# Exponentials as 32-bit integers, split into float16 halves for the product with v

## The chip, the cores and the metric

The kernel runs on one core of one Trainium2 chip. The metric is the device time of one execution in microseconds (us), the median of several runs. Times inside an execution come from one profiled execution and its trace.

## What is computed

Two parts follow each other: block-sparse attention over 4 batches, 8 heads, 768 positions and a head width of 64, and a mixture of experts in which each of 3072 rows goes to its best two of 8 experts.

```python
scores = scale * np.matmul(q, k.transpose(0, 1, 3, 2))      # scale = 1/8
scores = np.where(mask, scores, -1000000000.0)               # blocks of 32 x 32
scores = scores - np.max(scores, axis=-1, keepdims=True)
attn = np.exp(scores)
attn = attn / (np.sum(attn, axis=-1, keepdims=True) + 1e-09)
attn_out = np.matmul(attn, v)                                # (4, 8, 768, 64)
x = attn_out.transpose(0, 2, 1, 3).reshape(3072, 512)
# experts: the top 2 of x @ w_gate + log1p(exp(x @ w_noise)) * noise, softmax over the two,
# out[rows] += weight * (relu(x[rows] @ w1[e]) @ w2[e])
```

The change touches attention only.

## The kernel before

**Stages.** Attention is a loop of 192 steps (`steps`, 4 batches x 8 heads x 6 key tiles of 128; two heads make a group, so a group is 12 steps and there are 16 groups). Then the experts run unit by unit. The router of a batch works in the background of the attention steps, and some loads and conversions of the first expert's weights lie in the last steps.

**One attention step** n belongs to one head and one tile c of 128 keys. TensorE forms the scores of these 128 keys against all 768 queries in two halves of 384 (`exp`, called with x = 0 and 1). Each half is two float16 products added in PSUM: line 237 (high part of k and q, with what the split of k left over) and line 238 (k again, with what the split of q left over, the block mask, and one row that carries minus the row maximum and the constant LNS). ScalarE turns each half into exponentials (line 239), 128 x 384 float32, into half of a tile p32 of 128 x 6 x 128.

Ahead of that, the row maxima of a later head are found: `max_mm` (line 208) makes two products of width 384 into one of two PSUM buffers pm, and VectorE reduces them (`max_red`, line 215). At a head's last tile `max_end` (line 222) writes minus the maximum into a column of the natural-layout tile qb, which SyncE transposes into q2 (line 225).

Three steps after its exponentials (LA = 3), a tile's p32 is multiplied with v (`av`, line 259): p32's six blocks of 128 x 128 are the stationary weights, v's 128 x 65 the moving side, in float32, summed over the head's six steps in one PSUM buffer po. Column 65 is a constant, so that it collects the denominator. Behind a head's last step `av_end` copies po out (ScalarE, line 271), adds the 1e-9 (line 274), inverts (276), scales (279), and splits the result into two float16 parts (ScalarE line 286, GpSimd line 288).

**Splits and loads.** q and k come in as float32 (line 154, ScalarE's queue) and are split into two float16 parts: high on ScalarE (lines 173 and 177), the rest on GpSimd (175 and 179). v is loaded straight into its float32 tile vx (line 149, two transfers of 192 KB a group, since vx has 65 columns where v has 64).

**What sets the order.** The program is written out in the order in which each engine runs it; `steps` is that order. Within a step TensorE has: first score half, maxima product, second score half, product with v; in a head's last step of v the product comes first. VectorE has: line 274 if due, the maximum, lines 276, 279 and 222 if due, with the router's small instructions between (`background`). Each engine takes its own list in order; the engines wait for one another through semaphores, and for buffers: 3 of pe (scores), 2 of pm (maxima), 1 of po, 5 of p32.

Of the kernel before, what the change touches and what calls it, by code (L numbers as in the profile page):

```python
# [9 lines left out]
F32 = mybir.dt.float32  # L10
F16 = mybir.dt.float16
BF16 = mybir.dt.bfloat16
I32 = mybir.dt.int32
U32 = mybir.dt.uint32
AF = mybir.ActivationFunctionType
ALU = mybir.AluOpType
AX = mybir.AxisListType
PSUM = bass.MemoryType.PSUM
P = 128


LNS = 12.0 * math.log(2.0)

XS = 64.0
WS = 64.0
# [14 lines left out]
class Attention:  # L40
    G = 2
# [6 lines left out]
    VLOADAT = 6  # L48

    SPLITAT = ((0, 0, 0), (1, 0, 1), (2, 1, 0), (5, 1, 1), (5, 2, None), (6, 3, None), (8, 4, None), (9, 5, None))  # L50
    PPB = 5
    LA = 3

# [13 lines left out]
    def open(self, ctx, early):  # L67

        tc, nc, G, T = self.tc, self.nc, self.G, self.T
        pool = lambda c, name, bufs, **kw: c.enter_context(tc.tile_pool(name=name, bufs=bufs, **kw))  # L70
        self.const = pool(ctx, "aconst", 1, side="right")
        self.tp = pool(ctx, "atp", 3, side="right")
        self.pp = pool(ctx, "app", self.PPB, side="right")
        self.sm = pool(ctx, "asm", 4, side="right")
        self.xp = pool(ctx, "axp", 2, side="right")
        self.ps_e = pool(ctx, "ps_e", 3, space=PSUM)
        self.ps_m = pool(ctx, "ps_m", 2, space=PSUM)
        self.ps_o = pool(ctx, "ps_o", 1, space=PSUM)
        self.natp = pool(ctx, "anat", 1, side="right")
        self.raw = pool(early, "araw", 2)  # L80
        self.nat = [tuple(self.natp.tile([P, G, T, P], F16, name=f"{n}{i}") for n in ("ka", "qa", "qb"))
                    for i in range(2)]
        self.k2 = [self.natp.tile([P, G, T, P], F16, name=f"k2{i}") for i in range(3)]

        self.vx = [self.natp.tile([P, G, T, self.D + 1], F32, name=f"vx{i}") for i in range(3)]
        for t in self.vx:
            nc.gpsimd.memset(t[:, :, :, self.D:], 1.0 / XS)

    def masks(self, mi, sb):

        nc, T, NB, G = self.nc, self.T, self.NB, self.G
# [6 lines left out]
                       allow_small_or_imprecise_dtypes=True)  # L98
        self.kb = mi.tile([P, G, T, P], F16, name="kb")
        nc.gpsimd.memset(self.kb[:, :, :, 64:], 0.0)  # L100
        nc.gpsimd.memset(self.kb[:, :, :, 64 + NB:65 + NB], 64.0)
        self.blank(0)
        nc.vector.tensor_scalar(rowi, rowi, 5, None, op0=ALU.arith_shift_right)
        rowb = mi.tile([P, T], F32, name="rowb")
# [28 lines left out]
    def blank(self, i):  # L133
        ka, qa, qb = self.nat[i]
        self.nc.gpsimd.memset(qa[:, :, :, 64 + self.NB:], 0.0)
        self.nc.gpsimd.memset(qb[:, :, :, 64 + self.NB:], 0.0)

    def blocks(self, i, k):
        for g in range(self.G):
# [2 lines left out]
    def load(self, g, eng=None, names="kq"):  # L142
        b, h0 = divmod(g * self.G, self.H)
        r = self.st.setdefault(g, {})
        for nm in names:
            if nm == "v":
                x = r["v"] = self.vx[g % 3]
                for h in range(self.G):
                    (eng or self.nc.scalar).dma_start(x[:, h, :, 0:self.D],
                                                      self.v[b, h0 + h].rearrange("(p t) d -> p t d", p=P))  # L150
                continue
            src = {"k": self.k, "q": self.q}[nm]
            x = self.raw.tile([P, self.G, self.T * self.D], F32, name="raw_" + nm)
            (eng or self.nc.scalar).dma_start(x, src[b, h0:h0 + self.G].rearrange("h (p t) d -> p h (t d)", p=P))
            r[nm] = x.rearrange("p h (t d) -> p h t d", t=self.T)

    def new(self, r, nm):
        r[nm] = self.tp.tile([P, self.G, self.T, P], F16, name=nm)
# [58 lines left out]
    def max_end(self, n):  # L217
        g, h, t = self.where(n)
        r = self.st[g]
        if t == self.T - 1:  # L220
            qb = self.nat[g % 2][2]
            self.nc.vector.tensor_scalar(qb[:, h, :, 64 + self.NB], r["m", h], -1.0 / 64.0, LNS / 8.0,
                                         op0=ALU.mult, op1=ALU.add)
            d = r["q2", h] = self.tp.tile([P, self.T, P], F16, name="q2", bufs=2)
            self.later(self.Q2LATE, lambda: self.nc.sync.dma_start_transpose(
                out=d, in_=qb[:, h].rearrange("p t c -> p (t c)")))

    def exp(self, n, x):
        nc, T = self.nc, self.T
        g, h, c = self.where(n)  # L230
        r = self.st[g]
        if x == 0:
            self.st["p", n] = self.pp.tile([P, T, P], F32, name="p32")
        p32 = self.st["p", n]
        t = slice(3 * x, 3 * x + 3)
        pe = self.psum()
        nc.tensor.matmul(pe[:, 0:384], r["k1"][:, h, c, :], r["q1"][:, h, t, :], start=True, stop=False)  # L237
        nc.tensor.matmul(pe[:, 0:384], r["k2"][:, h, c, :], r["q2", h][:, t, :], start=False, stop=True)  # L238
        nc.scalar.activation(p32[:, t].rearrange("p t c -> p (t c)"), pe[:, 0:384], AF.Exp, scale=0.125)  # L239

    def flush(self):
        for n in sorted(self.todo):
# [9 lines left out]
    def av(self, n):  # L252
        g, h, c = self.where(n)
        r = self.st[g]
        if c == 0:
            r["o", h] = self.ps_o.tile([P, self.T, self.D + 1], F32, name="po")
        po, p32 = r["o", h], self.st.pop(("p", n))
        for t in range(self.T):
            self.nc.tensor.matmul(po[:, t, :], p32[:, t, :], r["v"][:, h, c, :], start=(c == 0 and t == 0),  # L259
                                  stop=(c == self.T - 1 and t == self.T - 1), skip_group_check=True)  # L260

    def av_end(self, n, part, on_group):

        nc, T, D, G = self.nc, self.T, self.D, self.G
        if n < 0 or n >= self.NSTEP or n % T != T - 1:
            return
        g, h, c = self.where(n)
        r = self.st[g]
        if part == "copy":
            xo = r["xo", h] = self.sm.tile([P, T, D + 1], F32, name="xo", bufs=2)  # L270
            nc.scalar.activation(xo, r.pop(("o", h)), AF.Copy)  # L271
        elif part == "sum":
            r["rc", h] = self.sm.tile([P, T], F32, name="rc")
            nc.vector.tensor_scalar(r["rc", h], r["xo", h][:, :, D], 1e-9 * math.exp(LNS) / XS, None, op0=ALU.add)
        elif part == "inverse":
            nc.vector.reciprocal(r["rc", h], r["rc", h])
        elif part == "scale":
# [14 lines left out]
    def start(self, mi):  # L292
        nc, D, NB = self.nc, self.D, self.NB
# [4 lines left out]
        r = self.st[0] = {nm: self.raw.tile([P, self.G, self.T, D], F32, name="raw_" + nm) for nm in "kq"}  # L298
# [4 lines left out]
        ka, qa, qb = self.nat[0]  # L303
# [24 lines left out]
            self.max_end(n)  # L328
        self.flush()
        self.load(0, nc.scalar, "v")  # L330
        self.split(1, 3)
        self.split(1, 2)
        nc.sync.dma_start(self.k2[1][D:], self.k2[0][D:])
# [10 lines left out]
    def steps(self, on_group, background):  # L344
        NSTEP, LM, LA, GT = self.NSTEP, self.LM, self.LA, self.G * self.T
        for n in range(NSTEP + LA + 6 + self.ROWLATE):
            g, i = divmod(n, GT)
# [24 lines left out]
                self.av(j)  # L372
            background(n, 0)
            self.av_end(j - 1, "sum", on_group)
            background(n, 1)
            for m in new:
                self.max_red(m)
# [722 lines left out]
```

## Time and profile before

| | |
|---|---|
| runs shown | 1116.45 us median of 3 (1113.26 to 1122.55) |
| profiled execution: span from the first to the last instruction | 1064.2 us |
| the profiled execution's own time | not recorded beside its span; the median of the runs is 52 us above it |
| attention: first and last product with v | 32.3 and 469.7 us |
| experts | from 469.9 us |
| granted TensorE clock, mean | 0.986 |
| DMA traffic | 156.24 MB, mean 147 GB/s |

How to read the rows. Engines are PE (TensorE's matmuls), PEld (its weight loads, which overlap PE), DVE (VectorE), ACT (ScalarE), POOL (GpSimd), SP (SyncE). A group's row gives line, engine, operation, tiles written and read, shape, count, busy us and mean ns of one, and then the idle time in front of it with what ended it. A timeline row gives start, length, engine, line, operation. A row of a stretch gives its limits and length, the busy us of the engines with their counts, the granted clock, the share of the 16 DMA engines and GB/s. A matmul's length includes a modelled end, so the pace of matmuls is read from their starts. A float32 matmul of the program is recorded as two loads and two matmuls.

### The profile page before, as it was taken

The numbers are of one execution on the slowest core, as the hardware profiler recorded it, in microseconds if no ns is written. First come the engines' busy times: TensorE is split into PE (matmuls) and PEld (weight loads), VectorE is DVE, ScalarE is ACT, GpSimd is POOL, SyncE is SP. The second block draws the span as 40 slices with busy tenths as digits, with TensorE's granted clock in tenths as the row PEclk, the third lists the DMA queues.
The fourth block names the chain that finished last, engine by engine and source line by source line (L and its number), as shares of the span: only waits on it lengthen the run. The fifth ranks groups of instructions, "written<-read, shape, count | busy, mean of one in ns | idle before, by whom it ended". The sixth has DMA issues, their size and how long they took to land. (4 is left out here: it accounts for less than half of the span.)

```text
span 1064.2 us, 18061 instructions
## 1 busy us (share of the span) xinstructions
PE 998.3 (94%) x7261; PEld 675.8 (64%) x7261; DVE 443.5 (42%) x831; ACT 362.9 (34%) x738; POOL 316.3 (30%) x378
## 2 busy tenths in 40 slices
PE   2999999999999999999787999999999999999993
PEld 1788888888888888886364545455555455554551
DVE  6544545555554556426413413424234143341220
ACT  2455555455555554444112303213023031230200
POOL 2122222342224315322444225133250241512211
PEclk9999999999999999999898999999999999999997
DMA  8979886576556756555687938729359185381200
GB/s 193 173 165 231 226 187 135 108 142 142 131 125 131 142 112 150 125 115 180 128 161 193 222 110 168 215 67 248 116 152 232 61 200 174 114 220 50 64 33 32
DMA packets 258798, 156.24 MB, mean 147 GB/s; under 512 B 197409, under 2 KB 234529, under 8 KB 258704
## 3 DMA queue, kind: packets, MB, share of 16 engines
q1 hardware_dynamic: 206816, 91.45, 41.3%
q0 software_dynamic: 14256, 39.58, 13.1%
q10 hardware_dynamic: 37632, 23.95, 8.1%
q8 instruction: 59, 0.97, 0.4%
q14 instruction: 35, 0.29, 0.1%
HBM read 79.62 MB, written 26.32 MB: 100 GB/s over the span
## 5 line engine op out<-in xcount | busy, mean ns | idle before, releaser
L259 PEld LDWEIGHTS po<-vx,p 128*128 128x128 f32 x2304 | 277.3, 191 | 11.1 <-ACT xo L271 0.6
L259 PE MATMUL po<-vx,p 128*128 128x65 f32 x2304 | 274.4, 271 | 0.0
L215 DVE TENSOR_REDUCE m<-pm 128x1 f32<-128x768 f32 x192 | 183.1, 956 | 186.4 <-PE pm L208 186.2
L239 ACT ACTIVATE p<-pe 128x384 f32<-128x384 f32 x384 | 183.2, 492 | 222.4 <-PE pe L238 211.0
L784 ACT ACTIVATE hh<-ph 128x408 f16<-128x408 f32 (+2 forms) x136 | 66.6, 490 | 334.7 <-PE ph L779 274.9
L829 POOL DMA_INDIRECT out_dram<-y,mt x56 | 59.8, 1067 | 321.8 <-DVE y L827 216.8
L799 PEld LDWEIGHTS <-hh 128*128 128x128 f16 x768 | 75.1, 98 | 94.8 <-issue 9.2
L238 PE MATMUL pe<-q,k 128*128 128x384 f16 x384 | 125.6, 327 | 6.3 <-DMA q<-qb 6.3
L237 PE MATMUL pe<-q,k 128*128 128x384 f16 x384 | 126.1, 328 | 3.0 <-DMA q<-q 1.6
L785 DVE SCALAR_TENSOR_TENSOR hl<-ph,hh 128x408 f16<-128x408 f32 (+2 forms) x136 | 75.9, 559 | 123.5 <-ACT hh L784 122.9
L779 PE MATMUL ph<-xta,w1hb 128*128 128x408 f16 x512 | 111.5, 341 | 12.4 <-DMA xta<-xg 8.3
L827 DVE SCALAR_TENSOR_TENSOR y<-py,mt,pv 128x512 f32<-128x512 f32 x48 | 36.0, 750 | 176.9 <-PE py L799 161.9
L208 PE MATMUL pm<-k,q 88*128 88x384 f16 x384 | 97.2, 337 | 12.1 <-DMA k<-kb 10.8
L779 PE MATMUL ph<-xtb,w1ha 128*128 128x408 f16 (+1 forms) x448 | 91.2, 325 | 3.8 <-DVE hl L785 2.5
L779 PEld LDWEIGHTS <-w1hb 128*128 128x128 f16 x512 | 50.5, 99 | 52.8 <-issue 15.4
L779 PEld LDWEIGHTS <-w1ha 128*128 128x128 f16 x576 | 56.1, 98 | 38.2 <-issue 3.0
L799 PE MATMUL py<-w2ha,hh 128*128 128x512 f16 x192 | 73.7, 384 | 6.4 <-DVE y L827 6.4
L288 POOL TENSOR_TENSOR x<-xr,x 128x384 f16<-128x384 f32 x32 | 29.2, 913 | 156.1 <-ACT x L286 156.0
L799 PE MATMUL py<-w2la,hh 128*128 128x512 f16 x192 | 73.6, 383 | 0.0
L799 PE MATMUL py<-w2ha,hl 128*128 128x512 f16 x192 | 73.5, 383 | 0.0
L799 PE MATMUL py<-w2hb,hh 128*128 128x512 f16 x192 | 72.8, 379 | 0.4 <-DVE y L827 0.4
L799 PE MATMUL py<-w2hb,hl 128*128 128x512 f16 x192 | 72.8, 379 | 0.1
(164 smaller groups left out, 1131.0 us busy)
## 6 DMA issues: line engine op xcount, KB each, us to landing
wraw<-in_moe_w_dram SPq DMA_DIRECT2D x64, 512.0 KB, 6.0
q<-q SPq DMA_DIRECT2D x32, 192.0 KB, 4.2
vx<-in_v_dram ACTq DMA_DIRECT2D x32, 192.0 KB, 3.9
x_rows<-x SPq DMA_DIRECT2D x16, 384.0 KB, 3.9
out_dram<-zero ACTq DMA_DIRECT2D x8, 768.0 KB, 4.2
raw_k<-in_k_dram ACTq DMA_DIRECT2D x14, 384.0 KB, 3.4
raw_q<-in_q_dram ACTq DMA_DIRECT2D x14, 384.0 KB, 4.2
k<-k SPq DMA_DIRECT2D x17, 192.0 KB, 4.3
```

Of the source, the lines that this page charges most:

```text
L208: self.nc.tensor.matmul(pm[:, c, 0:384], r["q3"][0:K, h, t, :], r["k2"][0:K, h, 3 * c:3 * c + 3, :], start=True, stop=True)
L215: self.nc.vector.tensor_reduce(self.st[g]["m", h][:, t:t + 1], pm[:, :, 0:384], axis=AX.XY, op=ALU.max)
L237: nc.tensor.matmul(pe[:, 0:384], r["k1"][:, h, c, :], r["q1"][:, h, t, :], start=True, stop=False)
L238: nc.tensor.matmul(pe[:, 0:384], r["k2"][:, h, c, :], r["q2", h][:, t, :], start=False, stop=True)
L239: nc.scalar.activation(p32[:, t].rearrange("p t c -> p (t c)"), pe[:, 0:384], AF.Exp, scale=0.125)
L259: self.nc.tensor.matmul(po[:, t, :], p32[:, t, :], r["v"][:, h, c, :], start=(c == 0 and t == 0), stop=(c == self.T - 1 and t == self.T - ...
L779: nc.tensor.matmul(ph[:, b, 0:m], w[wt][:, kb, fs], r["xt"][:, kb, a, o:o + m], start=i == 0, stop=i == last)
L784: nc.scalar.activation(hv, ph[:, b, 0:m], AF.Relu)
L785: nc.vector.scalar_tensor_tensor(self.hl[:, f, o:o + m], ph[:, b, 0:m], 0.0, hv, op0=ALU.max, op1=ALU.subtract)
L799: nc.tensor.matmul(py, h[:, f, o], w[x][:, f, :], start=i == 0, stop=i == last)
L827: nc.vector.scalar_tensor_tensor(y[0:m], py[0:m, 0:self.D], r["mt"].bitcast(F32)[0:m, c, 1:2], self.pv[0:m, c, :], op0=ALU.mult, op1=ALU.add)
L829: nc.gpsimd.indirect_dma_start(out=self.out, out_offset=bass.IndirectOffsetOnAxis(ap=r["mt"][0:m, c, 0:1], axis=0), in_=y[0:m], in_offset= ...
```

## The change

**What it does.** The exponential is scaled up (LNS from 8.32 to 18.69, now as a row of its own in qb that a row of 64 in kb multiplies) and written as a 32-bit integer, into a tile p32 from a new pool of three. `halve` reads this tile as 1536 16-bit integers and writes each times 2^-5 as float16: one VectorE instruction for each step, placed ahead of the step's maximum. v is loaded raw (one transfer of 384 KB a group) and `vsplit` makes three float16 tiles of it: vx = 1024 v (ScalarE), vl = what the rounding left (VectorE), vb = 2^-16 vx (GpSimd). `av` then has three float16 products in place of each float32 one: upper halves with vx, upper halves with vl, lower halves with vb. The upper halves are every second float16 of the tile, as are the lower ones.

```diff
+LNROW = 2.3359375
+LNS = 8.0 * LNROW
+HC = 2.0 ** -5
+LOW = 2.0 ** -16
+VS = 1024.0
...
+    VSPLITAT = ((6, 0), (7, 1), (7, 2))
...
+        self.pi = pool(ctx, "api", 3, side="right")
...
-        self.vx = [self.natp.tile([P, G, T, self.D + 1], F32, name=f"vx{i}") for i in range(3)]
-        for t in self.vx:
-            nc.gpsimd.memset(t[:, :, :, self.D:], 1.0 / XS)
+        self.vx = [self.natp.tile([P, G, T, self.D + 1], F16, name=f"vx{i}") for i in range(3)]
+        self.vb = [self.natp.tile([P, G, T, self.D + 1], F16, name=f"vb{i}") for i in range(3)]
+        self.vl = [self.natp.tile([P, G, T, self.D], F16, name=f"vl{i}") for i in range(3)]
+        for t, w in zip(self.vx + self.vb, [VS / XS] * 3 + [VS / XS * LOW] * 3):
+            nc.gpsimd.memset(t[:, :, :, self.D:], w)
...
-        nc.gpsimd.memset(self.kb[:, :, :, 64 + NB:65 + NB], 64.0)
+        nc.gpsimd.memset(self.kb[:, :, :, 64 + NB:66 + NB], 64.0)
...
+        self.nc.gpsimd.memset(qb[:, :, :, 65 + self.NB:66 + self.NB], LNROW)
...
             if nm == "v":
-                x = r["v"] = self.vx[g % 3]
-                for h in range(self.G):
-                    (eng or self.nc.scalar).dma_start(x[:, h, :, 0:self.D],
-                                                      self.v[b, h0 + h].rearrange("(p t) d -> p t d", p=P))
-                continue
-            src = {"k": self.k, "q": self.q}[nm]
+                r["v"] = self.vx[g % 3], self.vl[g % 3], self.vb[g % 3]
+            src = {"k": self.k, "q": self.q, "v": self.v}[nm]
             x = self.raw.tile([P, self.G, self.T * self.D], F32, name="raw_" + nm)
             (eng or self.nc.scalar).dma_start(x, src[b, h0:h0 + self.G].rearrange("h (p t) d -> p h (t d)", p=P))
...
+    def vsplit(self, g, part):
+        nc, D = self.nc, self.D
+        r = self.st[g]
+        vh, vl, vb = r["v"]
+        vh, vb = vh[:, :, :, 0:D], vb[:, :, :, 0:D]
+        if part == 0:
+            nc.scalar.activation(vh, r["raw_v"], AF.Copy, scale=VS)
+        elif part == 1:
+            m = lambda a: a.rearrange("p h t d -> p (h t) d")
+            nc.vector.scalar_tensor_tensor(m(vl), m(r["raw_v"]), VS, m(vh), op0=ALU.mult, op1=ALU.subtract)
+        else:
+            nc.gpsimd.tensor_scalar(vb, vh, LOW, 1.0, op0=ALU.mult, op1=ALU.mult)
...
-            self.st["p", n] = self.pp.tile([P, T, P], F32, name="p32")
-        p32 = self.st["p", n]
+            self.st["p32", n] = self.pi.tile([P, T, P], I32, name="p32")
+        p32 = self.st["p32", n]
...
+    def halve(self, n):
+        p32 = self.st.pop(("p32", n))
+        p = self.st["p", n] = self.pp.tile([P, self.T, P, 2], F16, name="p16")
+        self.nc.vector.tensor_scalar(p.rearrange("p t c w -> p (t c w)"), p32.bitcast(U16).rearrange("p t c -> p (t c)"),
+                                     HC, None, op0=ALU.mult)
...
         for t in range(self.T):
-            self.nc.tensor.matmul(po[:, t, :], p32[:, t, :], r["v"][:, h, c, :], start=(c == 0 and t == 0),
-                                  stop=(c == self.T - 1 and t == self.T - 1), skip_group_check=True)
+            first, last = c == 0 and t == 0, c == self.T - 1 and t == self.T - 1
+            for i, (o, w, v) in enumerate(((po[:, t, :], 1, vh[:, h, c, :]), (po[:, t, 0:D], 1, vl[:, h, c, :]),
+                                           (po[:, t, :], 0, vb[:, h, c, :]))):
+                self.nc.tensor.matmul(o, p[:, t, :, w], v, start=first and i == 0, stop=last and i == 2,
+                                      skip_group_check=True)
...
         self.load(0, nc.scalar, "v")
+        for i in range(3):
+            self.vsplit(0, i)
...
             self.av_end(j - 1, "sum", on_group)
+            if n < NSTEP:
+                self.halve(n)
             background(n, 1)
...
+            for at, part in self.VSPLITAT:
+                if i == at and g + 1 < self.NG:
+                    self.vsplit(g + 1, part)
```

**The order on the engines.** Where the order of one engine's instructions matters, here is the list before and after. The line numbers of the changed program differ: 227 is the maxima product (208 before), 255 and 256 the score products (237, 238), 288 the product with v (259), 234 the maximum (215), 241 the column of maxima (222), 257 the exponential (239), 262 the halving, 169 and 172 v's first and second part.

TensorE, at the product with v of one step and the score products behind it, before (one float32 row of the program stands for six blocks):

```order
L259 MATMUL po_454<-vx0_100,p32_372 128x65 x6
L237 LDWEIGHTS k1_156
L237 MATMUL pe_471<-q1_178,k1_156 128x384
L238 LDWEIGHTS k20_97
L238 MATMUL pe_471<-q2_292,k20_97 128x384
```

The same place now, from the last of the six blocks on:

```order
L288 LDWEIGHTS p16_294
L288 MATMUL po_337<-vx0_103,p16_294 128x65
L288 LDWEIGHTS p16_294
L288 MATMUL po_337<-vl0_109,p16_294 128x64
L288 LDWEIGHTS p16_294
L288 MATMUL po_337<-vb0_106,p16_294 128x65
L255 LDWEIGHTS k1_169
L255 MATMUL pe_398<-q1_191,k1_169 128x384
```

Each block has three loads and three products; the first two load the same columns again. What follows is as before.

VectorE, over some steps of attention, before:

```order
L215 TENSOR_REDUCE m_540<-pm_682 128x1
L222 TENSOR_SCALAR qb0_93<-m_540 128x6
L215 TENSOR_REDUCE m_710<-pm_711 128x1
L215 TENSOR_REDUCE m_710<-pm_741 128x1
L437 SCALAR_TENSOR_TENSOR r_whl_750<-r_wgn_588,r_whl_750 128x4x16
L274 TENSOR_SCALAR rc_773<-xo_739 128x6
L215 TENSOR_REDUCE m_710<-pm_759 128x1
```

And the same place now:

```order
L234 TENSOR_REDUCE m_706<-pm_918 128x1
L241 TENSOR_SCALAR qb0_96<-m_706 128x6
L262 TENSOR_SCALAR p16_987<-p32_956 128x1536
L234 TENSOR_REDUCE m_961<-pm_962 128x1
L172 SCALAR_TENSOR_TENSOR vl2_111<-raw_v_434,vx2_105 128x768
L262 TENSOR_SCALAR p16_1027<-p32_1013 128x1536
L234 TENSOR_REDUCE m_961<-pm_1020 128x1
L473 SCALAR_TENSOR_TENSOR r_whl_1031<-r_wgn_782,r_whl_1031 128x4x16
L303 TENSOR_SCALAR rc_1066<-xo_1018 128x6
L262 TENSOR_SCALAR p16_1068<-p32_1035 128x1536
L234 TENSOR_REDUCE m_961<-pm_1040 128x1
```

A halving stands ahead of each maximum, so a maximum now also waits until the step's second exponential is done; v's second part stands between two steps once in a group.

ScalarE at the start, from the split of group 1's q to the first exponential, before:

```order
L177 ACTIVATE qa1_95<-raw_q_167 128x12x64
L149 DMA vx0_100<-in_v_dram 128x6x64 x2
L154 DMA raw_k_240<-in_k_dram 128x2x384
L154 DMA raw_q_242<-in_q_dram 128x2x384
L239 ACTIVATE p32_244<-pe_245 128x384
```

And now:

```order
L196 ACTIVATE qa1_98<-raw_q_180 128x12x64
L160 DMA raw_v_240<-in_v_dram 128x2x384
L169 ACTIVATE vx0_103<-raw_v_240 128x12x64
L160 DMA raw_k_257<-in_k_dram 128x2x384
L160 DMA raw_q_259<-in_q_dram 128x2x384
L257 ACTIVATE p32_261<-pe_262 128x384
```

The conversion of the first v, which needs that v's load, stands between its issue and the issues of group 2's k and q.

More of the change, by code (lines that the diff above doesn't have):

```diff
@@ L14 @@
 U32 = mybir.dt.uint32
+U16 = mybir.dt.uint16
 AF = mybir.ActivationFunctionType
@@ L19 @@
 P = 128
-LNS = 12.0 * math.log(2.0)
+LNROW = 2.3359375
[3 more added lines that the diff above has]
+VS = 1024.0
 XS = 64.0
@@ L146, in load @@
             if nm == "v":
-                x = r["v"] = self.vx[g % 3]
-                for h in range(self.G):
-                    (eng or self.nc.scalar).dma_start(x[:, h, :, 0:self.D],
-                                                      self.v[b, h0 + h].rearrange("(p t) d -> p t d", p=P))
-                continue
-            src = {"k": self.k, "q": self.q}[nm]
+                r["v"] = self.vx[g % 3], self.vl[g % 3], self.vb[g % 3]
+            src = {"k": self.k, "q": self.q, "v": self.v}[nm]
             x = self.raw.tile([P, self.G, self.T * self.D], F32, name="raw_" + nm)
             (eng or self.nc.scalar).dma_start(x, src[b, h0:h0 + self.G].rearrange("h (p t) d -> p h (t d)", p=P))
-            r[nm] = x.rearrange("p h (t d) -> p h t d", t=self.T)
+            r["raw_v" if nm == "v" else nm] = x.rearrange("p h (t d) -> p h t d", t=self.T)
+    def vsplit(self, g, part):
[10 more added lines that the diff above has]
+            nc.gpsimd.tensor_scalar(vb, vh, LOW, 1.0, op0=ALU.mult, op1=ALU.mult)
     def new(self, r, nm):
@@ L221, in max_end @@
             qb = self.nat[g % 2][2]
-            self.nc.vector.tensor_scalar(qb[:, h, :, 64 + self.NB], r["m", h], -1.0 / 64.0, LNS / 8.0,
-                                         op0=ALU.mult, op1=ALU.add)
+            self.nc.vector.tensor_scalar(qb[:, h, :, 64 + self.NB], r["m", h], -1.0 / 64.0, None, op0=ALU.mult)
             d = r["q2", h] = self.tp.tile([P, self.T, P], F16, name="q2", bufs=2)
@@ L256, in av @@
             r["o", h] = self.ps_o.tile([P, self.T, self.D + 1], F32, name="po")
-        po, p32 = r["o", h], self.st.pop(("p", n))
+        po, p = r["o", h], self.st.pop(("p", n))
+        vh, vl, vb = r["v"]
+        D = self.D
         for t in range(self.T):
-            self.nc.tensor.matmul(po[:, t, :], p32[:, t, :], r["v"][:, h, c, :], start=(c == 0 and t == 0),
-                                  stop=(c == self.T - 1 and t == self.T - 1), skip_group_check=True)
+            first, last = c == 0 and t == 0, c == self.T - 1 and t == self.T - 1
[3 more added lines that the diff above has]
+                                      skip_group_check=True)
     def av_end(self, n, part, on_group):
@@ L273, in av_end @@
             r["rc", h] = self.sm.tile([P, T], F32, name="rc")
-            nc.vector.tensor_scalar(r["rc", h], r["xo", h][:, :, D], 1e-9 * math.exp(LNS) / XS, None, op0=ALU.add)
+            nc.vector.tensor_scalar(r["rc", h], r["xo", h][:, :, D], 1e-9 * math.exp(LNS) * LOW * HC * VS / XS, None, op0=ALU.add)
         elif part == "inverse":
```

## The prediction

> **What bounds the kernel now.** I read the page's busy times first, then the stretch from 100 to 400 us, which is attention alone: once whole, once for the row maxima of line 215.
>
> ```profile
> PE 998.3 (94%) x7261; PEld 675.8 (64%) x7261; DVE 443.5 (42%) x831; ACT 362.9 (34%) x738; POOL 316.3 (30%) x378
> 100.00:400.00 300.00, 298.58 (x2490) 253.93 (x2489) 159.21 (x341) 156.34 (x359) 83.01 (x112) 1.00 0.68 145
> 100.00:400.00 300.00, 123.43 (x129) 1.00 0.68 145
> L259 PEld LDWEIGHTS po<-vx,p x2304: 186/192/192, 32.3 to 469.7; 128*128 128x128 f32 x192
> DVE m L215 <- PE pm L208: 133.4, 104, 2.6
> ACT p L239 <- PE pe L238: 138.5, 114, 2.5
> ```
>
> In the second row the columns after the 300 us are PE, PEld, DVE, ACT, POOL, then clock, DMA share and GB/s: PE is busy 298.58 of 300 us at clock 1.00. The waits of the same stretch say it again: VectorE and ScalarE spend their idle time waiting for a matmul. So TensorE sets the pace of attention. The weight loads of line 259 run from 32.3 to 469.7 us: 437.4 us for 192 steps, or 2.278 us a step. The stretch holds 300 / 2.278 = 131.7 steps, so VectorE works 159.21 / 131.7 = 1.21 us a step (0.94 on maxima, 0.27 on all else) and ScalarE 1.19.
>
> One step of the timeline shows what TensorE does in it.
>
> ```profile
> 300.67 0.49 PE L208 MATMUL pm<-k,q 88*128 88x384 f16 x2
> 301.00 0.33 PE L237 MATMUL pe<-q,k 128*128 128x384 f16 x1
> 301.17 0.32 PE L238 MATMUL pe<-q,k 128*128 128x384 f16 x1
> 301.33 1.45 PE L259 MATMUL po<-vx,p 128*128 128x65 f32 x12
> 302.61 0.33 PE L237 MATMUL pe<-q,k 128*128 128x384 f16 x1
> ```
>
> A row's length includes the pipeline's end, so I go from start to start. The six products of width 384 start 0.165 us apart (300.67 to 301.00 for two): 0.99 us. The six float32 products with v, recorded as twelve pairs of load and matmul, take 302.61 - 301.33 = 1.28 us, 107 ns a pair. Together 2.27: the step.
>
> **The change on TensorE.** It removes the 12 float32 pairs and adds 18 float16 pairs of width 64 or 65. Float16 pairs so narrow stand in the trace at two other places: 48 in a row in the router, and the unit of 96 rows among the experts.
>
> ```profile
> 165.07 0.18 PE L477 MATMUL pe<-r_whl,r_xT 128*128 128x32 f16 x1
> ...
> 166.25 0.17 PE L479 MATMUL pe<-r_whl,r_xT 128*128 128x16 f16 x1
> 545.89 0.21 PE L808 MATMUL py<-hh,w2ha 128*128 128x96 f16 x1
> ...
> 546.78 0.21 PE L808 MATMUL py<-hh,w2ha 128*128 128x96 f16 x1
> ```
>
> Widths 32 and 16: 1.18 us / 47 = 25 ns a pair. Width 96: 0.89 / 21 = 42 ns. Width 65 lies between; I take 30 ns, so 18 x 30 = 0.54 us, and TensorE's step becomes 0.99 + 0.54 = 1.53 us.
>
> One thing no row shows: all those weights are contiguous, and the new ones are every second float16 of a tile (p[:, t, :, w]). Its bounds are 25 ns, if only the type counts, and the 107 ns of the float32 load, whose 128 columns lie 4 bytes apart as the new ones do. I take 30, since the type is what separates the two rows.
> The Trainium skill ("TensorE: Matmul & The Clock Gate", section "Weight-path perf modes") says that fast weight load works for 128 columns of any type but float32, at column steps up to 1,024 elements; by that the sum stays as it is. The same section says the fast load reads 32 bits at a time, two bfloat16 values, and half of each read would be wasted here; if that doubles a load to 50 ns, the 18 cost 0.90 us and the step 1.89, still under VectorE's below. No run here shows a strided load.
>
> **The change on VectorE.** Each step gains one instruction over 1536 elements, uint16 to float16. Three rows price it.
>
> ```profile
> L126 DVE TENSOR_TENSOR t<-sbf,rowb 128x432 f32<-128x432 f32 x1 | 0.6, 609 | 0.0
> L114 DVE TENSOR_TENSOR al<-t 128x144 f32<-128x144 f32 x1 | 0.3, 307 | 0.0
> L115 DVE TENSOR_SCALAR al<-al 128x144 f32<-128x144 f32 x1 | 0.2, 234 | 0.0
> L420 DVE TENSOR_SCALAR r_tri<-r_d 128x128 f16<-128x128 int32 x1 | 0.2, 215 | 0.0
> ```
>
> The first two differ by 288 elements and 302 ns: 1.05 ns an element, 156 ns fixed. The third does 144 in 234 - 156 = 78 ns: an instruction with one tensor input, SBUF to SBUF, goes at twice that rate, and the fourth (215 ns) shows the same with a conversion. Three prices follow. At one element a tick 1536 x 1.05 + 156 = 1.77 us; at two, as these rows count elements, 0.96; and by bytes, since the rows read 8 bytes in the time in which the tile's 3072 bytes are 384 such readings, 384 x 1.05 + 156 = 0.56. I take 0.56, because the rows at the double rate all have 4-byte input, and keep the others for the range and the rivals.
> The Trainium skill ("VectorE: DVE Perf Modes", section "The perf-mode tier table") gives tensor_scalar a fourfold mode when everything is 16-bit in SBUF, which is 0.56 too; if only its float32 column, 2x, applied to integers, the step would be that of the first rival.
>
> Instructions in a row overlap at their ends: two maxima of 0.96 take 1.82.
>
> ```profile
> 42.86 1.82 DVE L215 TENSOR_REDUCE m<-pm 128x1 f32<-128x768 f32 x2 [1.30 <-PE pm L208]
> ```
>
> So each following one costs about 0.09 less: 0.87 for the maximum, 0.47 for the halving. Rows for v's second part and for what stands in the way:
>
> ```profile
> L693 DVE SCALAR_TENSOR_TENSOR w2la<-wraw,w2ha 128x1024 f16<-128x1024 f32 x16 | 19.5, 1222 | 14.5 <-ACT w2ha L692 14.5
> 16.33 0.84 ACT L177 ACTIVATE qa<-raw_q 128x768 f16<-128x768 f32 x1 [2.35 <-DMA raw_q<-in_q_dram]
> 17.25 1.64 POOL L179 TENSOR_TENSOR qb<-raw_q,qa 128x768 f16<-128x768 f32 x1 [1.54 <-ACT qa L177]
> 17.53 1.85 DVE L222 TENSOR_SCALAR qb<-m 128x6 f16<-128x6 f32 x1
> L222 DVE TENSOR_SCALAR qb<-m x32: 163/182/1848, 17.5 to 443.4; 128x6 f16<-128x6 f32 x32
> L288 POOL TENSOR_TENSOR x<-xr,x 128x384 f16<-128x384 f32 x32 | 29.2, 913 | 156.1 <-ACT x L286 156.0
> ```
>
> From the 1222 ns of 1024 elements, v's 768 cost 156 + 768 x 1.04 = 0.95 us once in 12 steps: 0.08 a step. ScalarE's part of v is the 0.84 us of line 177 (0.07 a step, giving 1.26, off the path); GpSimd's is at most the 1.64 of line 179, with nothing urgent queued behind it. The exponential now writes int32; I keep line 239's price, since ScalarE has 0.7 us of slack a step.
>
> The L222 rows are a warning. An instruction of six elements, usually 182 ns, took 1.85 us at 17.53, until the GpSimd instruction that began at 17.25 ended (18.89): a one-input VectorE instruction on SBUF waits out a GpSimd one. The halving is of this kind. GpSimd has six of 0.91 us and now one of up to 1.64 in 12 steps. With steps of 1.94 us, a 0.91 meets a halving's start with a chance of 0.91 / 1.94 and then holds it 0.46 us: 0.21 each; the long one 0.69. (6 x 0.21 + 0.69) / 12 = 0.16 us a step.
>
> VectorE's step: 0.87 + 0.47 + 0.27 + 0.08 + 0.16 = 1.85 us. That is above TensorE's 1.53 and ScalarE's 1.26, so **VectorE takes over the pace**. There is also a ring: the two maxima buffers let product n+2 start only after maximum n; then come the maxima product and the second score product (0.49 + 0.33), an exponential (0.49), the halving (0.56), the maximum (0.96), with hand-overs about 2.95 us for two steps, 1.48 a step. It does not bind but leaves little slack when VectorE's extras fall together; for that I add 0.09. Step: 1.94.
>
> **The sum.** (2.278 - 1.94) x 192 = 65 us. The start gives back some: v is now loaded raw and converted, and the loads of the next k and q stand behind that conversion in ScalarE's queue. They were issued at 18.47; a v load lands in 3.9 us (median) from its issue at 16.33, and the conversion takes 0.84, so they go out about 3 us later. (The 32 v loads of 192 KB become 16 of 384 KB, in longer runs; I credit nothing for that.)
>
> ```profile
> vx<-in_v_dram ACTq DMA_DIRECT2D x32, 192.0 KB, 3.9
> 80.00:100.00 20.00, 20.00 (x163) 17.29 (x163) 9.34 (x14) 10.43 (x24) 5.43 (x6) 1.00 0.97 226
> ```
>
> The first reader of those loads sits at 28.16 us, so perhaps nothing is lost; with DMA at a share of 0.97 around 80 to 100 us I take 5 us off in all. The experts' part starts when attention ends and is shifted as a whole: the waits for their weights and rows stay. So 1064.2 - 60 = 1004 us of span. The median of the runs, 1116.45, is 52 us above the span, and I carry that unchanged: **1056 us**.
>
> **Rivals.**
> 1. The halving runs at two elements a tick. VectorE: 0.87 + 0.87 + 0.27 + 0.08 + 0.18 + 0.09 = 2.36 us a step, 0.08 more than now: + 16, so 1132 us. For it: every fast row has exactly this rate. Against: all of them have 4-byte input. It decides from a halving of 0.90 us up (0.81 behind another instruction), where the sum reaches 2.278.
> 2. The strided weight load has no fast path: 18 x 107 = 1.92 us, TensorE's step 2.91, + 0.63 x 192 = 121: 1237 us, **slower**. Its place is line 259's successor; it decides from (2.278 - 0.99) / 18 = 72 ns a pair. For it: the new columns lie 4 bytes apart like the float32 ones. Against: the type is float16, whose loads pace at 25 ns.
> 3. The halving runs at one element a tick: 0.87 + 1.68 + 0.27 + 0.08 = 2.90 us a step, again some 1236 us. Against: line 115 and line 420.
> 4. Nothing is gained, because DMA holds the step. Its share is 0.68 at 2.278 us, 1.55 us of work a step; at 1.94 us that is 0.80, but the stretch quoted above stands at 0.97 already. If steps 14 to 55, which carry the zero fill, kept their pace, 41 x 0.34 = 14 us of the gain would go: 1070, within my range; if all steps did, 1116.
>
> **How the numbers follow.** The forecast with its variants (DMA, a load of 50 ns, more or fewer lock waits) 0.72; rival 1 0.12; rival 2 0.07; rival 3 0.05; no gain 0.04. The likeliest's own range is 1025 (steps of 1.80 us, no lock, (2.278 - 1.80) x 192 = 92) to 1085. The range for 8 in 10 reaches to rival 1: 1025 to 1132, leaving out rivals 2 and 3 and a tail below. About 1% is what a measurement of this kernel can tell from no change: faster by over 1% 0.72; within 1% the 0.04 and a third of rival 1, 0.08; slower the rest of it with rivals 2 and 3, 0.20.
>
> **What would show it.** Right: the halving at about 0.56 us (some at 1 us or more, against a GpSimd row); pairs of the product with v starting some 30 ns apart; VectorE at 90% or more of an attention stretch, PE near 80%, and maxima that no longer wait for line 208's product but follow the halving; the last product with v near 405 us instead of 470. Wrong: a halving near 0.96 or 1.77; pairs at 50 ns or more; VectorE with idle time that ends on an ACT row, which would mean that the ring and not the work paces it; or an experts' part that grows by what attention loses.

## The result and the profile after

The changed kernel takes **1053.2 us** (median of 4 runs, 1047.26 to 1060.0) where the kernel before takes 1114.86 (4 runs): ratio 0.943, 95% interval 0.937 to 0.949. The prediction was 1056, range 1025 to 1132. Chips differ here: in the four calls the kernel before took 1114.86, 1066.9, 1124.8 and 1069.5 us, so a whole time is compared with runs of its own call only; parts of a trace are compared across calls where that is said. Medians are of all runs of a kernel, ratios leave out runs more than 1.5% above the fastest of their kernel, and the traces of e11 and e12 come from such runs.

In the changed program the maximum's product and reduction are lines 227 and 234, the write of the maximum 241, the scores 255 and 256, the exponential 257, the halving 262, the product with v 288, v's three parts 169, 172 and 174, and the load and conversion of the experts' weights 721, 728 and 729.

First the page of after: its engines, and four groups of attention (count, then busy us and mean ns of one, then idle time in front and what ended it).

```profile
PE 897.5 (85%) x8413; PEld 531.8 (51%) x8413; DVE 549.4 (52%) x1039; ACT 372.8 (35%) x754; POOL 340.9 (32%) x399
L234 DVE TENSOR_REDUCE m<-pm 128x1 f32<-128x768 f32 x192 | 181.9, 950 | 1.4 <-PE pm L227 1.4
L227 PE MATMUL pm<-k,q 88*128 88x384 f16 x384 | 99.3, 343 | 65.3 <-DVE m L234 38.0
L262 DVE TENSOR_SCALAR p<-p 128x1536 f16<-128x1536 uint16 x192 | 115.6, 602 | 62.8 <-ACT p L257 49.7
L288 PE MATMUL po<-vx,p 128*128 128x65 f16 x1152 | 126.2, 198 | 0.5 <-DVE p L262 0.4
```

VectorE went from 443.5 to 549.4 us busy and TensorE from 998.3 to 897.5. Before, the maximum waited for its product; now the product waits for the maximum (line 227 behind line 234). The line of the halving and one step's products with v:

```profile
L262 DVE TENSOR_SCALAR p<-p x192: 543/555/1506, 24.9 to 423.5; 128x1536 f16<-128x1536 uint16 x192
```

```profile
252.32 0.19 PE L288 MATMUL po<-vx,p 128*128 128x65 f16 x1
252.35 0.19 PE L288 MATMUL po<-vl,p 128*128 128x64 f16 x1
252.38 0.19 PE L288 MATMUL po<-vb,p 128*128 128x65 f16 x1
...
252.84 0.19 PE L288 MATMUL po<-vb,p 128*128 128x65 f16 x1
252.87 0.33 PE L255 MATMUL pe<-q,k 128*128 128x384 f16 x1
```

The halving takes 0.555 us (median). Eighteen pairs take 252.87 - 252.32 = 0.55 us, 30.6 ns a pair.

For the pace I cut out the same 144 steps in every trace, from the first exponential of step 24 to that of step 168. Rows of that stretch: limits, length, then busy PE, PEld, DVE, ACT, POOL, the clock, DMA share and GB/s. Before:

```profile
81.57:414.86 333.29, 331.87 (x2759) 282.30 (x2758) 178.81 (x384) 172.90 (x396) 92.33 (x125) 1.00 0.70 150
```

After:

```profile
72.95:364.50 291.55, 240.28 (x3621) 168.26 (x3621) 255.78 (x541) 179.39 (x409) 107.24 (x135) 0.98 0.87 175
```

A step fell from 2.315 to 2.025 us. TensorE was busy for 99.6% of the stretch and is for 82%; VectorE is busy for 88% (1.776 us a step) and idle 0.25 us a step. Attention as a whole, first to last product with v, went from 437.6 to 391.8 us (33.4 to 425.2). These two traces need not be of like chips; the pairs below are.

### The profile page after: what moved, and what is told of

Same layout as the page of the kernel before. It is cut to its first block, busy times and chain, and to the rows that moved or that the text cites. A ratio compares the mean times of both kernels' runs of the same rounds, so it can differ in the third digit from the quotient of the medians.

```text
span 1052.9 us, 20575 instructions
## 1 busy us (share of the span) xinstructions
PE 897.5 (85%) x8413; PEld 531.8 (51%) x8413; DVE 549.4 (52%) x1039; ACT 372.8 (35%) x754; POOL 340.9 (32%) x399
## 5 line engine op out<-in xcount | busy, mean ns | idle before, releaser
L257 ACT ACTIVATE p<-pe 128x384 int32<-128x384 f32 x384 | 182.4, 492 | 155.2 <-PE pe L256 128.1
L262 DVE TENSOR_SCALAR p<-p 128x1536 f16<-128x1536 uint16 x192 | 115.6, 602 | 62.8 <-ACT p L257 49.7
L288 PEld LDWEIGHTS <-p 128*128 128x128 f16 x3456 | 131.6, 100 | 27.6 <-issue 6.8
L255 PE MATMUL pe<-q,k 128*128 128x384 f16 x384 | 129.8, 338 | 13.0 <-ACT p L257 6.3
L256 PE MATMUL pe<-q,k 128*128 128x384 f16 x384 | 129.1, 336 | 8.4 <-DMA q<-qb 8.2
L288 PE MATMUL po<-vl,p 128*128 128x64 f16 x1152 | 126.4, 196 | 1.9 <-issue 1.9
L288 PE MATMUL po<-vb,p 128*128 128x65 f16 x1152 | 126.6, 197 | 1.5 <-issue 1.5
L288 PE MATMUL po<-vx,p 128*128 128x65 f16 x1152 | 126.2, 198 | 0.5 <-DVE p L262 0.4
L815 PE MATMUL ph<-xtb,w1ha 128*128 128x408 f16 (+1 forms) x448 | 97.1, 337 | 21.6 <-DVE hl L821 16.5
L227 PEld LDWEIGHTS <-q 88*128 88x128 f16 x384 | 37.9, 100 | 120.4 <-issue 94.1
L815 PEld LDWEIGHTS <-w1ha 128*128 128x128 f16 x576 | 57.7, 101 | 61.7 <-issue 28.1
```

Of the source, the lines that this page charges most:

```text
L227: self.nc.tensor.matmul(pm[:, c, 0:384], r["q3"][0:K, h, t, :], r["k2"][0:K, h, 3 * c:3 * c + 3, :], start=True, stop=True)
L262: self.nc.vector.tensor_scalar(p.rearrange("p t c w -> p (t c w)"), p32.bitcast(U16).rearrange("p t c -> p (t c)"), HC, None, op0=ALU.mult)
L288: self.nc.tensor.matmul(o, p[:, t, :, w], v, start=first and i == 0, stop=last and i == 2, skip_group_check=True)
L815: nc.tensor.matmul(ph[:, b, 0:m], w[wt][:, kb, fs], r["xt"][:, kb, a, o:o + m], start=i == 0, stop=i == last)
```

## The experiments

My theory was that VectorE's work, with what GpSimd holds up of it, now paces attention. The rivals: the halving's place makes the stages wait in turn, TensorE's time still counts in full, the strided loads cost something, or transfers are late.

**Before and change again.** Four runs edit nothing. They show what a chip alone does.

> The kernel before, unchanged, for a second trace. The prediction carried 52 us between span and median as something outside the span. If that is right, the span is again near 1064 us with a time near 1116. The rival: the first profiled execution was an unusually quick one, and the time is span plus some 2 us as for the changed kernel; then the span is near 1112, with attention at about 440 to 460 us and the rest in the experts' part, which would then hold the same stalls of TensorE that the changed kernel shows there.

> The kernel before, unchanged, for its parts on the chip of this call. On the chip of the two profiles of before so far (1064 us) attention took 436 us and the part behind it 594; the changed kernel was profiled on a chip on which before takes 1115 to 1125 us, and there the experts' part took 623 to 628 us. Theory (the second chip is slower in both parts): if before takes 1110 us or more here, the experts' part is 620 us or more and attention 450 us or more. Rival (the 50 us lie outside the span): span 1064 as before, and the time 50 us longer. If before takes about 1066 us here, the run repeats 436 and 594 within 3 us.

> The change itself, on the chip of the runs that follow, as their base. If the ratio of 0.943 belongs to the change, it comes out again. The rival: the kernel before took 1115 us beside the first run of the change and 1067 beside the later experiments, so the ratio holds a chip's part; attention went from some 437 us to 392, and 45 us off a kernel of 1067 would be a ratio near 0.96.

> The change, unchanged, beside the other kernels of this call. If before takes 1110 us or more here: ratio 0.93 to 0.95, attention 388 to 392 us. If before takes about 1066 us: the theory that the gain lies in attention and the chips differ outside it expects a ratio of 0.955 to 0.965 (1019 to 1030 us), attention 385 to 392 us, the experts' part 594 to 600 us. The rival, that part of the gain of 6 per cent belonged to the slow chip alone, expects a ratio of 0.97 or more.

Measured: before 1064.22 and 1066.11 us, with spans of 1062.4 and 1064.3, attention 436.1 and 441.1, the experts 594.3 and 591.2. The change: 1047.77 us, ratio 0.937 [0.928, 0.946], beside a before of 1124.8; and 1016.5, ratio 0.954 [0.945, 0.964], beside 1069.5. The 144 steps of before (e9), of the change beside 1124.8 (e5), and beside 1069.5 (e10):

```profile
84.65:417.94 333.29, 331.87 (x2759) 282.28 (x2758) 178.88 (x384) 172.90 (x396) 92.33 (x125) 1.00 0.72 151
```

```profile
72.99:362.10 289.11, 240.94 (x3621) 168.49 (x3621) 255.81 (x541) 179.63 (x408) 107.37 (x135) 0.98 0.89 177
```

```profile
74.32:363.44 289.12, 238.88 (x3621) 167.01 (x3621) 255.60 (x541) 179.86 (x408) 107.11 (x135) 0.99 0.88 177
```

The change's middle is the same on both chips to 0.01 us: 2.008 us a step. So close an agreement is chance, for the run of after took 2.4 us more (291.55); a difference of that size says nothing. The two differ in the last 24 steps (61.1 us in e5, 48.7 in e10) and in the experts (622.9 and 603.2). Every profiled execution took 1.7 to 1.9 us more than its span, and so did the runs of before at 1125 us (1124.8 with a span of 1123.0), so no part of 50 us lies outside the span. On one chip, e9 to e10, the span fell by 49.0 us: attention -63.2 (441.1 to 377.9), its start +2.2, the experts +12.0. Against the attention of the other two traces of before (436.1 and 437.6) the gain would be 58 to 60. Before was never profiled on a chip of 1115 us; where its extra 50 us lie stays open. The record shows only a lower granted clock there: 0.944 to 0.977 over the seven runs beside e5, 0.977 to 0.988 over the fourteen beside e1 and e9.

Of the expectations, e1 met neither of its two readings, since the run itself was quick, and e9's attention lies 5 us above the expected 436, where 3 were allowed. In e10 attention came out 7 us under the expected 385 to 392 and the experts 3 us over 594 to 600, while the ratio fits.

**Loads side by side.** As many products of the same sizes, with the weights' columns next to each other (so they multiply other numbers than the result needs):

```diff
-                self.nc.tensor.matmul(o, p[:, t, :, w], v, ...
+                self.nc.tensor.matmul(o, p[:, t].rearrange("p c w -> p (c w)")[:, w * P:(w + 1) * P], v, ...
```

> The change with contiguous weights: each load takes 128 neighbouring float16 values of the tile instead of every second one (the products are wrong). If a strided load costs nothing, the pairs start 29 to 31 ns apart as in the change, and attention takes the same 390 us within 5. The rival, that the stride costs something that the starts hide: pairs 25 to 27 ns apart and a shorter attention.

Measured 1049.28 us, attention 387.8 against 389.9 in e5 of the same call; the 144 steps 288.41 against 289.11, and 18 pairs take 0.54 to 0.56 us as before. The stride costs nothing that can be seen. The Trainium skill ("TensorE: Matmul & The Clock Gate", "Weight-path perf modes") says that fast load covers 128 columns of any type but float32 at such steps; the traces agree, 30.6 ns strided against 107 ns for float32. The doubling that I had considered for half-wasted reads does not show.

**Halving twice.** A second, identical halving into a tile that nobody reads:

```diff
+        again = self.pi.tile([P, self.T, P, 2], F16, name="again", bufs=1)
+        self.nc.vector.tensor_scalar(again..., p32.bitcast(U16)..., HC, None, op0=ALU.mult)
```

> A second, identical halving into a scratch tile in each step. If VectorE's work sets attention's pace, each adds its 0.47 us: 192 x 0.47 = 90 us more, near 1143, with attention at about 480 us. The rival, that something else paces and VectorE has 0.2 us of room a step: at most 50 us more.

```profile
86.44:429.62 343.18, 245.14 (x3621) 166.43 (x3621) 338.48 (x685) 184.08 (x408) 115.74 (x134) 1.00 0.72 149
```

Measured 1085.62 us, attention 448.0. Against e10, on another chip of like speed, VectorE gained 338.48 - 255.60 = 82.9 us of work in the middle and the time grew by 54.1; the rest went into VectorE's idle time, which fell from 33.5 to 4.7 us. Attention as a whole grew by 70.1 us against e10, between the 90 expected and the 50 of the rival. So with VectorE busy for 98.6% of the middle its work sets the pace; about a third of what was added had found room before that.

**Fewer products.** Without the product with vl (e4, the first added line), and with only the one with vx (e12, the second):

```diff
-            for i, (o, w, v) in enumerate(((po[:, t, :], 1, vh[:, h, c, :]), (po[:, t, 0:D], 1, vl[:, h, c, :]),
-                                           (po[:, t, :], 0, vb[:, h, c, :]))):
+            for i, (o, w, v) in enumerate(((po[:, t, :], 1, vh[:, h, c, :]), (po[:, t, :], 0, vb[:, h, c, :]))):
+            for i, (o, w, v) in enumerate(((po[:, t, :], 1, vh[:, h, c, :]),)):
```

> The product of the upper halves with v's second part is left out, so 12 pairs of load and matmul a step instead of 18. If VectorE paces attention, TensorE only idles more: within 1% of the change's 1053, at most 10 us faster. The rival, that TensorE is still on the path: 192 x 6 x 0.03 = 35 us faster, near 1018.

> The change with only the first of the three products with v left (the low part of v and the low half of the exponentials are not added, so the result is rougher). TensorE's step falls from 1.54 us to 0.99 + 6 x 0.031 = 1.17 us; VectorE's, ScalarE's and GpSimd's work stays. Theory (VectorE with its lock and its waits for the exponentials paces the step): attention 366 to 380 us, at most 25 us below the change of this call, since what goes is the part of TensorE in the waits. Rival (TensorE and VectorE take turns in the ring, so that TensorE's time counts in full): 0.37 us a step, 70 us less, attention 315 to 325 us. With two products it took 369.2 us on the other kind of chip.

Measured: 1025.79 us, ratio 0.962 [0.953, 0.971], attention 369.2; and 1016.78, ratio 0.946 [0.936, 0.956], attention 367.4. The 144 steps of e12:

```profile
76.19:359.50 283.31, 211.64 (x1893) 122.72 (x1893) 256.02 (x541) 179.70 (x409) 106.87 (x134) 0.92 0.88 180
```

Removing 12 pairs a step, 12 x 30.6 ns x 144 = 53 us of TensorE's work, shortened the middle by 5.8 us (4.7 in e4). TensorE doesn't pace the step; a tenth of the removed time shows. The test is weaker than its count, because the clock fell to 0.92: TensorE's busy time fell by 27.2 us (238.88 to 211.64), not 53. In e4, where the clock was 0.96, it fell by 15.2. The shorter attention of e4 did not shorten the whole: its ratio, 0.962, is not below the change's 0.954 in e10, and the part behind attention took 609.3 us against 603.2.

**Halving behind the maximum.** The order on VectorE turned round, and then (e7) the same with GpSimd's instructions of the splits cut to 4 of 64 columns (the other columns keep what an earlier group left). The edit of the order:

```diff
-            if n < NSTEP:
-                self.halve(n)
             background(n, 1)
             for m in new:
                 self.max_red(m)
+            if n < NSTEP:
+                self.halve(n)
```

> The halving stands behind the step's maximum instead of ahead of it. If VectorE paces attention and its 63 us of idle time in front of the halvings come from the order (the halving waits for the step's second exponential while a maximum that is ready stands behind it), most of that goes: 30 to 55 us faster than the change, near 1000 to 1025. The rival, that TensorE, ScalarE or the instruction supply are late and VectorE only shows it: the idle time moves ahead of the maxima, and the time is within 1% of the change's 1053.

> The halving behind the maximum, and GpSimd's instructions on k, q and v's third part cut to 4 of 64 columns from the steps on (the other columns keep what an earlier group left: part of the result is wrong). With the halving behind the maximum the halving takes 679 ns on average and at the least some 545: if the difference is the wait for GpSimd, the mean falls to 590 or less and attention gets some 15 to 20 us shorter than the 379 us of the run with the halving behind the maximum. The rival, that the longer halvings have another cause or that the ring paces attention: within 5 us.

Measured: e2 1018.45 us, ratio 0.955 [0.945, 0.964], which is the change's own 0.954 (that it lies in the expected 1000 to 1025 is the chip's doing); e7 1047.66, 0.934 [0.926, 0.942], against the change's 0.937. The 144 steps of each:

```profile
70.14:366.46 296.32, 244.57 (x3621) 171.29 (x3621) 273.18 (x541) 179.62 (x409) 113.41 (x134) 0.97 0.87 173
```

```profile
70.13:361.30 291.17, 241.47 (x3621) 171.28 (x3621) 257.60 (x542) 177.38 (x410) 71.87 (x135) 0.96 0.93 176
```

The order by itself gains nothing: the middle takes 7.2 us more than in e10, and VectorE spends 17.6 us more on the same instructions (273.18 against 255.60), with a halving of 679 ns in the mean against 606. Taking 41.5 us of GpSimd's work away takes 15.6 of them back (e7 ran on the other chip, but the middles of the change agree there), though the halving stays at 633 ns, where 590 or less was expected. Every halving of e7 above 0.7 us still overlaps a row of GpSimd, most often line 318, the second part of attention's result (line 317 in the change):

```profile
223.46 0.91 POOL L318 TENSOR_TENSOR x<-xr,x 128x384 f16<-128x384 f32 x1 [2.69 <-ACT x L316]
...
223.60 1.19 DVE L263 TENSOR_SCALAR p<-p 128x1536 f16<-128x1536 uint16 x1
```

The halving ends 0.42 us behind GpSimd's instruction: it stood until that was done. So GpSimd's hold is real; the splits' share of it is 0.11 us of VectorE's time a step in this order. It is not 0.11 us of pace: the middle fell by 5.2 us only (296.32 to 291.17), since VectorE's idle time grew from 23.1 to 33.6. At 88% VectorE's work doesn't count in full. The Trainium skill ("SBUF — State Buffer", "Who interferes with whom") names VectorE's two-port modes and GpSimd as sharing a port pair under a lock; halvings of up to 2.27 us in e2 agree.

**The split of v earlier, then the transposes earlier.** e6 is e2 with v's parts made a group earlier. Its reason is a row of after that I had not foreseen, from the waits on SyncE's queue between 350 and 400 us:

```profile
SPq L721 <- DVE vl L172: 22.7, 1, 22.7
```

The experts' first weights go where the raw v was, so their load waits until the last group's v is split (steps 174 and 175), and the conversions of these weights stand in ScalarE's list ahead of exponentials. In e10, the change on the other chip:

```profile
382.33 0.94 DVE L172 SCALAR_TENSOR_TENSOR vl<-raw_v,vx 128x768 f16<-128x768 f32 x1
...
383.36 1.50 SPq L721 DMA_DIRECT2D wraw<-in_moe_w_dram  x3
...
386.87 1.06 ACT L728 ACTIVATE w1ha<-wraw 128x1024 f16<-128x1024 f32 x1 [8.88 <-DMA wraw<-in_moe_w_dram]
387.83 0.47 ACT L257 ACTIVATE p<-pe 128x384 int32<-128x384 f32 x1
...
388.35 0.48 PE L255 MATMUL pe<-q,k 128*128 128x384 f16 x1 [5.40 <-ACT p L257]
```

ScalarE stands 8.88 us for the weights, TensorE 5.40 behind it. e11 adds to e6 that k and q are transposed and copied up to three steps earlier, because in e6 TensorE still waited for a copy of k.

```diff
-                if i == at and g + 1 < self.NG:
-                    self.vsplit(g + 1, part)
+                if i == at and g == 0:
+                    self.vsplit(1, part)
+            for at, part in ((10, 0), (11, 1), (11, 2)):
+                if i == at and g + 2 < self.NG:
+                    self.vsplit(g + 2, part)
...
-    SPLITAT = ((0, 0, 0), (1, 0, 1), (2, 1, 0), (5, 1, 1), (5, 2, None), (6, 3, None), (8, 4, None), (9, 5, None))
+    SPLITAT = ((0, 0, 0), (1, 0, 1), (2, 1, 0), (3, 1, 1), (3, 2, None), (4, 3, None), (5, 4, None), (6, 5, None))
```

> The halving behind the maximum, and v of a group split in the group two ahead of its use, four steps behind its load, so that the last raw v is read some 8 steps earlier. In the change, SyncE stood 22.7 us in front of the first weight load, for VectorE's split of the last v (both tiles lie in the same memory), then ScalarE stood 6 us and TensorE 5 us for those weights. If that is the cause, the stop of 5 to 9 us before attention's end goes and the run is 6 to 12 us under the one with the halving behind the maximum alone. The rival, that the weights come late because the DMA queues are full: the stop stays.

> Three edits on the change: the halving behind the maximum's reductions, the split of v a group earlier (both were tried), and now the transposes and copies of k and q issued up to three steps earlier within the group. With the first two alone TensorE still waited 24.6 us in seven pieces for a copy of k; attention took 372.4 us on the slow kind of chip. If those waits were late issue, they go down to under 8 us, attention to 350 to 362 us, the ratio to 0.905 to 0.915 where before takes 1110 us or more (0.93 to 0.945 where it takes about 1066 us). Rival: the transfers are slow because the DMA queues are full, so the waits only move; attention stays at 368 to 376 us.

Measured: e6 1032.49 us, ratio 0.921 [0.912, 0.929], attention 372.4, 17.5 less than the change of the same call, and 1.5% below its median. e11 999.48, ratio **0.935 [0.927, 0.944]**, attention 360.9, 17.0 less than the change of its call: the lowest time, 1.7% below the change's median. The two were not run in one call, so which is faster is not shown; e2 was not run beside e6 either, so e6 is compared with the change. The two gains are of equal size, but lie in different places: e6's is 17.2 us in the last 24 steps, e11's 12.1 in the middle and 5.7 in the last 24. The 144 steps of e6, with its waits in them for copies and for the maximum:

```profile
71.45:364.60 293.15, 242.29 (x3621) 170.51 (x3621) 265.49 (x541) 179.61 (x408) 113.15 (x134) 0.96 0.87 175
```

```profile
PE pm L227 <- DVE m L234: 22.0, 30, 1.8
PE pm L227 <- DMA k<-k: 19.2, 6, 4.2
```

And e11:

```profile
75.76:352.75 276.99, 238.31 (x3621) 168.82 (x3620) 265.03 (x536) 180.41 (x408) 112.89 (x134) 0.98 0.85 183
```

```profile
PE pm L227 <- DVE m L234: 26.9, 42, 1.6
PE pe L256 <- DMA q<-qb: 9.7, 7, 3.3
```

e6's middle is no shorter than the change's (293.15 against 289.11); its last 24 steps take 43.9 us against 61.1. e11 keeps that (42.95) and takes 16.2 us out of the middle against e6, and VectorE is busy 96% of it. The 19.2 us of waits for k's copy are gone; those for the maximum's transpose rose from 3.0 to 9.7. That e11's theory held is read from the middles, which agree between chips for the change; its band of 350 to 362 us alone would not show it. The earlier transposes without the halving's move were not tried.

## Why the prediction came right

**Who paces.** Right in the main. TensorE was the bound and no longer is (82% busy; e12 gains a tenth of what it removes). VectorE is the busiest engine, and its work is the pace once its idle time is gone (e3). In the change itself it is busy for 88% of the middle, short of the 90% named as a sign, and 15.6 us less of work gave 5.2 (e7): its work and its waits pace the step together.

**TensorE's 30 ns a pair and 1.53 us a step.** Right: 30.6 ns, strided or not (e8). Rival 2 is out.

**The halving's 0.56 us.** Right: 0.555 median, 0.602 mean. Rivals 1 and 3 are out. The Trainium skill's table ("VectorE: DVE Perf Modes", "The perf-mode tier table") gives tensor_scalar a fourfold mode for bfloat16 in SBUF; the trace agrees from uint16 to float16, since 0.555 us is the prediction's price of 0.56, four elements where its first row does one.

**VectorE's 1.94 us a step.** The sum is near, 2.008 in e5 and e10, but by luck: two of its terms are off and cancel. Work was predicted at 1.85 with 0.16 of holding by GpSimd, and is 255.60 / 144 = 1.775: halvings above 0.55 us add up to 10.9 us in e10, 0.06 a step. The 0.09 for idle time is 0.23. I had worked out that idle from a ring that "does not bind" and looked at no queue. About two thirds of it (some 18 to 20 us of the 29 in the row below) comes within 3 us of a product for which TensorE had waited for a copy of k or q, and issuing these earlier takes it from (293.15 - 265.49) / 144 = 0.19 in e6 to (276.99 - 265.03) / 144 = 0.08 in e11. So the mark that I had set for a ring, VectorE idle until an ACT row, did appear and had another cause in the main; what fills the other third is not shown. In e10:

```profile
DVE p L262 <- ACT p L257: 29.2, 22, 2.7
```

**65 us from the steps.** On the chip of e9 and e10 63.2, near in sum. The forecast takes 0.34 us off each of 192 steps; its 2.278 is a mean over all steps, where its own row of 129 maxima in 300 us makes 2.33. The middle gave 44.2, 0.31 a step, and the first steps, to step 24, 12.5 (52.65 to 40.12 us from the first product with v; before took only 49.1 there, so some 3.5 of this is e9's own); the last 24 gave 6.5 (55.16 to 48.66), though TensorE stands still there for 5.4 us behind the load that waits for v's split. On the chip of after they took 60.7, more than the 55.16 of before on the other. The last product with v, predicted near 405 us, came at 412.1 and 425.2.

**5 us off for start and DMA.** Too little, and rival 4 was right in part. The start cost 2.2 us (32.0 to 34.2). Rival 4 had put up to 14 us on steps 14 to 55, which carry the zero fill. Here are these steps in e9, e10 and e11, and steps 55 to 168 of e10:

```profile
63.25:155.10 91.85, 91.85 (x728) 77.82 (x726) 46.30 (x73) 48.93 (x112) 19.67 (x23) 1.00 0.89 209
56.49:142.21 85.72, 68.55 (x969) 47.03 (x968) 67.45 (x116) 51.54 (x116) 24.76 (x32) 0.96 1.10 231
56.08:138.38 82.30, 68.43 (x966) 48.31 (x965) 72.08 (x113) 50.19 (x115) 25.27 (x32) 0.94 1.04 243
142.21:363.45 221.24, 185.95 (x2876) 130.53 (x2874) 204.65 (x456) 140.68 (x323) 88.89 (x116) 1.00 0.81 159
```

They gained 6.1 us of the 14 (2.7 in after), with the DMA share above 1 as the profile counts it, and VectorE idle 0.45 us a step. Behind step 55 the step is 221.24 / 113 = 1.96 us, close to the forecast, and VectorE is busy for 92.5%. So about 8 us of the gain went where rival 4 had put it. Whether it is a limit of the transfers or their late issue is not separated: e11 moves 243 GB/s in these steps where the change moves 231, so 231 was no limit, but it takes only 3.4 us out of them.

**The experts are shifted as a whole.** This failed. On one chip they took 603.2 us against 591.2, a fifth of what attention gained. The runs with a still shorter attention took longer there yet (e4 609.3, e11 611.6, e12 615.8; e2 has 596.3). TensorE's waits for the second part of the hidden rows grew from 7.3 us in e9 to 11.2 in e10; no experiment here settles why.

**52 us between span and median, carried unchanged.** This failed as a step: the profiled runs of e1 and e9 took 1.8 us more than their spans. The 52 us were another chip's, as far as the record shows. The forecast of 1056 was made from that chip's median and a gain worked out on a trace of another kind, and it came within 3 us by luck: by the medians the gain was 61.7 us beside after, 77.0 beside e5 and 53.0 beside e10.

## What to carry to other kernels

When a bound engine is relieved, price the next engine's work, and then its idle time as well, by itself in the stretch where the transfers are dense: ask for each transfer and each load how many steps ahead of its reader it is issued, since a slower loop had hidden that lateness. A buffer whose last reader changes delays whatever is loaded there next. Before adding up a span and a median, make sure that both are of one chip.

## What the runs showed of the hardware

**The clock.** TensorE's clock falls although no pause is long. In e12's 144 steps the granted clock is 0.92, where e10 has 0.99 with more work, and the longest pause there is 2.5 us; e4 has 0.96 and also at most 2.5. The waits of e12, one of its pauses, of 1.83 us, and the six us behind that, at clock 0.50:

```profile
PE pm L227 <- DVE m L234: 54.1, 77, 2.5
PE pm L227 <- DMA k<-k: 6.6, 4, 2.4
```

```profile
279.72 0.80 PE L227 MATMUL pm<-k,q 88*128 88x384 f16 x2 [1.83 <-DVE m L234]
```

```profile
279.50:285.50 6.00, 5.78 (x29) 3.02 (x29) 5.64 (x11) 2.35 (x5) 5.01 (x8) 0.50 0.40 48
```

The Trainium skill ("TensorE: Matmul & The Clock Gate", "HAM oscillation — how this bites in real kernels") puts the limit at gaps above about 3.4 us; here the clock fell to half behind shorter ones. In the last 24 steps the change ran at 0.80 (after) and 0.89 (e10), and e11 at 1.00:

```profile
364.50:425.20 60.70, 44.94 (x607) 30.79 (x607) 32.70 (x58) 26.12 (x58) 23.72 (x33) 0.80 0.52 114
```

```profile
352.75:395.70 42.95, 36.06 (x606) 26.47 (x605) 36.21 (x59) 25.53 (x59) 24.55 (x33) 1.00 0.66 137
```

So a pause costs twice: TensorE's busy time for the same 606 or 607 matmuls is 44.94 us in the first row and 36.06 in the second. Within one call it is 44.35 at clock 0.80 in e5, and 37.09 at 1.00 in e6, where the longest stop of e5, 5.24 us, is gone.

**Types.** An exponential written as int32 takes 0.49 us, as it did in float32, and a float16 to float16 tensor_scalar of 768 elements on GpSimd 0.83 to 1.60 us.
